# Zero-tile matmuls between score visits, and another spread of the dense units over the first two batches

## The chip, the cores and the metric

The kernel runs on one core of a Trainium2 chip. The metric is the device time of one execution in microseconds (us). The engines are named as the profile names them: PE is TensorE's matmuls and PEld its weight loads, DVE is VectorE, ACT is ScalarE, POOL is GpSimd, SP is SyncE.

## The reference

The input is attention data for 8 batches, 12 heads, 448 positions and 64 elements a head, followed by a dense block with 768 inputs, 2048 hidden elements and 768 outputs. Cut to what is computed:

```python
scores = scale * np.matmul(q, k.transpose(0, 1, 3, 2)) - np.log(S)
attn = 1.0 / (1.0 + np.exp(-scores))
attn_out = np.matmul(attn, v)
x = attn_out.transpose(0, 2, 1, 3).reshape(B * S, H * D)
h = x @ w_in
g = h * (1.0 / (1.0 + np.exp(-beta * h)))
out = g @ w_out
```

The attention uses a sigmoid, not a softmax, so scores can be weighed as soon as they stand. `q`, `k` and `v` are drawn at a tenth of a standard normal deviate, and the output is 3584 x 768 in float32.

## The kernel before

**Names.** Four heads of one batch make a group `g`; a batch has `QPB` = 3 groups, and there are 24 of them. A slot `s` is two heads. The keys of a slot stand in `JF` = 3 full tiles of 128 and one of 64. `visit(g, jt)` (L211) computes the scores of a group's two slots against key tile `jt`: matmuls of `score` (L187) into two PSUM tiles `sco`, and then a sigmoid over each tile by ScalarE (`weigh`, L199), which makes `attnT`. The last key tile of two groups is done in one visit, as in (4, 3, (5,)). `half_visit` (L227) does the same for one half of the queries (224 of 448) and for two key tiles at a time. `attend` (L245) multiplies `attnT` with `v` and lets VectorE copy the result into `xT` (L265). `transpose` (L163) turns a group's `q` or `k` on VectorE, from `raw`, into which `load_one` (L92) brings it by a DMA of GpSimd's queue.

**Dense units.** The dense block is cut into units that fill TensorE's time between visits. `dense1` (L270) is one tile of 128 hidden elements: six matmuls, a sigmoid of ScalarE into `sg` (L284) and a product of VectorE into `gt` (L287). In the first batch it works on half of the positions (224 columns), later on all 448. It needs the column chunk of `w_in` that holds its tile: eight chunks of 256 columns, so two units use one chunk. `dense2` (L291) is 128 output rows by half of the output columns: sixteen matmuls, a copy of VectorE into `osb` (L308), and a store from SyncE's queue when a row is complete. The units stand in one list, `fill`, in a fixed order; `fill_units(n)` takes the next n of them.

**PSUM.** In the first part there are three score tiles of two banks each and two single banks; after `firsts.close()` (L410) two score tiles and four single banks, which the attends and the dense units share. Two score tiles are what one visit fills.

**The order** is written out by hand, and each engine works through its instructions in that order:

- GpSimd's queue loads q and k of the first three groups, `v` of batch 0, the second halves of q, the eight chunks of `w_in`, q and k of group 3, the first half of `w_out`'s columns in two transfers, `v` of batch 1, q and k of group 4, the second half of `w_out`, q and k of group 5.
- TensorE runs 11 matmuls on a tile of zeros, `still`, into the tile `idle` (L370), while the first loads are under way.
- First pass (L386): six `half_visit`s on the first half of the queries of groups 0 to 2, with `attend(0)` cut in two around the last of them. Then the attends of groups 1 and 2, with both half visits of group 0's second half between them (L393 to L408).
- Second pass (L412): four dense units; then for groups 1 and 2 and both halves of a visit: a half visit, half an attend of the group before, three dense units (L417). Then the last attend, the transposes of group 3, and four dense units.
- From there (L433) whole visits. A planner gives each visit a budget of dense work: `spread` names the first eleven, an equal share `rest` follows. Costs are counted as 0.58 for half a `dense1`, 1.13 for a whole one and 2.57 for a `dense2`. A unit is taken when half its cost still fits; a `dense1` of a later batch only when that batch's attends are behind. The transposes of the next group follow the visits with `jt` 1 and 2 (L443), and the attend of a group stands ahead of the next group's first visit (L436).

Of the kernel before, what the change touches and what calls it, by code (L numbers as in the profile page):

```python
# [13 lines left out]
def kernel(  # L14
# [10 lines left out]
    nc = tc.nc  # L25
# [6 lines left out]
    P = 128  # L32
# [4 lines left out]
    JF = S // P  # L37
# [3 lines left out]
    QPB = H // HQ  # L41
# [9 lines left out]
    NQUAD = B * QPB  # L51
# [40 lines left out]
    def load_one(g: int, r: int, c0: int = 0, c1: int = NB):  # L92
        b, t = divmod(g, QPB)
        if g not in raws:
            raws[g] = rawp.tile([P, 2, NB, D], FP16, tag="raw", name="raw")
        nc.gpsimd.dma_start(  # L96
            out=raws[g][:, r, c0:c1].rearrange("p c d -> p (c d)"),
            in_=(q, k)[r][b, HQ * t : HQ * (t + 1)].rearrange("h (p c) d -> (h p) (c d)", c=NB)[
                :, c0 * D : c1 * D
            ],  # L100
        )

    def load_qk(g: int):
        load_one(g, 0)
        load_one(g, 1)
# [4 lines left out]
    def last_base(s: int) -> int:  # L110
        return (s % 2 ^ swapped(s // 2)) * KL

    def load_v(b: int):
        vs[b] = vp.tile([P, H, JF + 1, D], FP16, tag="v16", name="v16")
        rows = v[b].rearrange("h (p c) d -> p h (c d)", c=NB)
        for i in range(HQ):
            nc.gpsimd.dma_start(  # L117
                out=vs[b][i * BLK : (i + 1) * BLK, :, 0:JF].rearrange("p h j d -> p h (j d)"),
                in_=rows[:, :, JF * i * D : JF * (i + 1) * D],
            )  # L120
        if b > 0:
            load_v_last(b)
# [36 lines left out]
    def in_order(b: int, t):  # L159
        t = t.rearrange("p c e -> p (c e)").bitcast(FP32)  # L160
        return t.rearrange("p (q c) -> p c q", c=NB) if b == B - 1 else t

    def transpose(g: int, r: int, c0: int = 0, c1: int = NB):  # L163
        raw = raws[g][:, r]
        if r == 0:
            if g not in qT:
                qT[g] = qTp.tile([P, NB * BLK, PAIR], FP16, tag="qT", name="qT")
            nc.vector.transpose(  # L168
                out=in_order(g // QPB, qT[g][:, c0 * BLK : c1 * BLK]),
                in_=raw[:, c0:c1].rearrange("p c d -> p (c d)").bitcast(FP32),  # L170
            )
            return
        kT[g] = kTp.tile([P, S, PAIR], FP16, tag="kT", name="kT")
        to = kT[g].rearrange("p k e -> p (k e)").bitcast(FP32)
        frm = raw.rearrange("p c d -> p (c d)").bitcast(FP32).rearrange("p (c f) -> p c f", c=NB)
        nc.vector.transpose(  # L176
            out=to[:, 0 : JF * P].rearrange("p (j i q) -> p i j q", j=JF, i=HQ),
            in_=frm[:, 0:NF].rearrange("p (i j) f -> p i j f", j=JF),
        )
        nc.vector.transpose(  # L180
            out=to[:, JF * P :], in_=frm[:, NF:].rearrange("p c f -> p (c f)")
        )
# [62 lines left out]
    def attend(g: int, c0: int, n: int, part=(0, 1)):  # L245
        b, t = divmod(g, QPB)
        if b not in xTs:
            xTs[b] = xTp.tile([P, NHC, S], FP16, tag="xT", name="xT")
        slots = [2 * g + x for x in part]
        avs = [psum["one"].tile([P, S], FP32, tag="one", name="av_ps") for _ in slots]  # L250
        todo = [(s, av, jt) for s, av in zip(slots, avs) for jt in range(JF)]
        for s, av, jt in todo + [(s, av, JF) for s, av in zip(slots, avs)]:
            at = at_tiles.pop((s, jt, c0))
            base, nk = (last_base(s), KL) if jt == JF else (0, P)
            for hh in range(2):
                nc.tensor.matmul(  # L256
                    av[hh * D : (hh + 1) * D, 0:n],
                    vs[b][base : base + nk, 2 * (s % NPAIR) + hh, jt],
                    at[base : base + nk, hh, 0:n],
                    start=(jt == 0),  # L260
                    stop=(jt == JF),
                    tile_position=(base, hh * D),
                )
        for s, av in zip(slots, avs):
            nc.vector.tensor_copy(out=xTs[b][:, s % NPAIR, c0 : c0 + n], in_=av[:, 0:n])  # L265
# [63 lines left out]
    M1_US, M1H_US, M2_US = 1.13, 0.58, 2.57  # L329
# [21 lines left out]
    def fill_units(n: int):  # L351
        for _ in range(n):
            fill[at_fill[0]][2]()
            at_fill[0] += 1
# [4 lines left out]
    with tc.manual_schedule():  # L359
        load_one(0, 0, 0, NH)  # L360
        load_one(0, 1)
        nc.gpsimd.memset(nlogs, NEG_LOG_S)
        nc.gpsimd.memset(dummy, 0.0)
        nc.scalar.activation(out=dummy, in_=dummy, func=AF.Sigmoid, bias=0.0, scale=1.0)

        still = const.tile([P, 512], FP16, name="still")
        nc.vector.memset(still, 0.0)  # L367
        nc.vector.memset(beta_in, 0.0)
        idle = psum["one"].tile([P, 512], FP32, tag="one", name="idle_ps")
        for _ in range(11):  # L370
            nc.tensor.matmul(idle, still[:, 0:P], still, start=True, stop=True)  # L371
        for g in range(1, QPB):
            load_one(g, 0, 0, NH)
            load_one(g, 1)
        load_v(0)
        load_v_last(0)
        nc.sync.dma_start(out=beta_in[0:NDC], in_=moe_beta.rearrange("(c p) -> c p", p=P))
        for g in range(QPB):
            load_one(g, 0, NH, NB)
        for c in range(WCH):  # L380
            load_w_in(c)
        for g in range(QPB):
            transpose(g, 0, 0, NH)
            transpose(g, 1)

        for g in range(QPB):  # L386
            for second in range(2):
                half_visit(g, 0, second)
                if g == QPB - 1:
                    attend(0, 0, QH, (second,))  # L390
        for g in range(QPB):
            transpose(g, 0, NH, NB)
        attend(1, 0, QH, (0,))  # L393
        half_visit(0, QH, 0)
        attend(1, 0, QH, (1,))
        for i in range(P // BLK):
            part = slice(i * BLK, (i + 1) * BLK)
            nc.vector.transpose(out=beta_sb[part], in_=beta_in[:, part])
        attend(2, 0, QH)
        load_qk(3)  # L400
        load_w_out(0, 0)
        load_w_out(1, 0)
        load_v(1)
        load_qk(4)
        load_w_out(0, 1)
        load_w_out(1, 1)
        load_qk(5)
        half_visit(0, QH, 1)  # L408

        firsts.close()  # L410
        share_psum(ctx, 2, 4)
        fill_units(4)  # L412
        for g in range(1, QPB):
            for second in range(2):
                half_visit(g, QH, second)
                attend(g - 1, QH, QH, (second,))
                fill_units(3)  # L417
        attend(QPB - 1, QH, QH)
        transpose(QPB, 0)
        transpose(QPB, 1)  # L420
        fill_units(4)

        visits = [(QPB, jt, ()) for jt in range(JF + 1)]
        for g in range(QPB + 1, NQUAD, 2):
            visits += [(g, jt, ()) for jt in range(JF)] + [(g, JF, (g + 1,))]
            visits += [(g + 1, jt, ()) for jt in range(JF)]
        spread = [3 * M1H_US] * 2 + [M2_US] + [3 * M1H_US] * 2 + [5 * M2_US / 6] * 6

        total = sum(u[0] for u in fill[at_fill[0] :])
        tail = 16 * M1_US + 10 * M2_US  # L430
        rest = (total - sum(spread) - tail) / (len(visits) - len(spread))
        budget, spent = 0.0, 0.0
        for i, (g, jt, also) in enumerate(visits):  # L433
            if jt == 0:
                if g > QPB:
                    attend(g - 1, 0, S)  # L436
                if g + 2 < NQUAD:
                    if g + 2 not in raws:
                        load_qk(g + 2)
                    if (g + 2) % QPB == 0:  # L440
                        load_v((g + 2) // QPB)
            visit(g, jt, also)
            if jt in (1, 2) and g + 1 < NQUAD:  # L443
                transpose(g + 1, jt - 1)
            budget += spread[i] if i < len(spread) else rest
            while at_fill[0] < len(fill):
                cost, ready, _ = fill[at_fill[0]]
                if ready > g or spent + cost / 2 > budget:
                    break
                spent += cost  # L450
                fill_units(1)
        attend(NQUAD - 1, 0, S)
        fill_units(len(fill) - at_fill[0])
# [30 lines left out]
```

## Time and profile before

Three runs took 406.98, 407.15 and 409.64 us; their median is 407.15. The profiled execution took 407.82 us, and its span, from the first to the last instruction, is 406.05 us. Its mean granted TensorE clock is 0.983.

| what | busy us | share of the span | instructions |
|---|---|---|---|
| PE | 395.8 | 97% | 3067 |
| PEld | 201.1 | 50% | 3067 |
| ACT | 236.7 | 58% | 317 |
| DVE | 169.9 | 42% | 335 |
| POOL | 77.2 | 19% | 133 |

The largest groups of TensorE are `dense1` (L276: 864 matmuls, 154.5 us), `dense2` (L298: 896 matmuls, 152.7 us), the scores (L190: 864 matmuls, 54.7 us) and the attends (L256: 432 matmuls, 44.1 us). The sigmoids over scores (L201) are 171 instructions and 160.7 us of ScalarE. The zero matmuls (L371) are 11 and take 4.0 us.

The page has the span in 40 equal slices of some 10 us. A digit is the busy share in tenths, PEclk the TensorE clock that was granted:

```profile
PE   5899999999999999999999999999999999999996
ACT  4778965587534784477643776457843677415400
PEclk9579999999999999999999999999999999999999
DMA  8999999991329402592229212492042200111022
```

TensorE is short of work only in the first slices, the clock is below its full value in slices 1 to 3, and the DMA engines are full for the first 90 us, in which all weights and the first batches are loaded.

The chain that ended last, by engine and by line, is TensorE's for the most part; the DMA share of it lies before 63 us:

```profile
PE 83%; DMA 12%; POOL 2%; issue 1%; DVE 1%; DVEq 0%; POOLq 0%
```

### The profile page before, as it was taken

To read this page: it belongs to the slowest core of one execution; us is meant where nothing else is said; L and a number is where in the kernel's file an instruction comes from. 1 tells how busy PE (TensorE), PEld (TensorE's weight loads), DVE (VectorE), ACT (ScalarE), POOL (GpSimd) and SP (SyncE) were. 2 spreads that over 40 slices of the span, in tenths; PEclk is the share of its full clock that TensorE was granted. 3 is DMA by queue.
4 is the path that set the end of the run, shared out by engine and by line. 5 is a ranking of instruction groups with operands and counts; after the bars stand their busy time and mean duration, and the time that the engine had idled before them with its cause. 6 is when DMAs were issued, how large, how long until landed. Compare 5 with 4: busy or idle time off the path is not lost.

```text
span 406.0 us, 7393 instructions
## 1 busy us (share of the span) xinstructions
PE 395.8 (97%) x3067; PEld 201.1 (50%) x3067; DVE 169.9 (42%) x335; ACT 236.7 (58%) x317; POOL 77.2 (19%) x133
## 2 busy tenths in 40 slices
PE   5899999999999999999999999999999999999996
PEld 2367654444554445444455444544445544555563
DVE  2245353355423653345522454235542365225421
ACT  4778965587534784477643776457843677415400
POOL 7833435420114110420105101321100000000000
PEclk9579999999999999999999999999999999999999
DMA  8999999991329402592229212492042200111022
GB/s 119 151 188 203 180 180 182 196 128 31 85 44 168 75 4 53 115 117 45 39 64 182 56 31 48 77 164 47 0 86 56 62 2 0 40 40 40 0 79 77
DMA packets 48801, 35.09 MB, mean 86 GB/s; under 512 B 28272, under 2 KB 45184, under 8 KB 48768
## 3 DMA queue, kind: packets, MB, share of 16 engines
q0 software_dynamic: 43376, 23.60, 44.8%
q1 hardware_dynamic: 5392, 11.02, 9.8%
q8 instruction: 24, 0.39, 0.4%
q14 instruction: 9, 0.07, 0.1%
HBM read 47.19 MB, written 11.01 MB: 143 GB/s over the span
## 4 chain that ended last, share of the span: by engine, by line
PE 83%; DMA 12%; POOL 2%; issue 1%; DVE 1%; DVEq 0%; POOLq 0%
PE m_ps L298 35%; PE m_ps L276 32%; PE sco L190 9%; PE av_ps L256 8%; DMA w_out<-in_moe_w_out_dram 4%; DMA raw<-in_q_dram 3%; DMA w_in<-in_moe_w_in_dram 3%; DMA v<-in_v_dram 2%; POOL raw L96 1%; POOL w_in L138 1%; POOL v L117 0%; DVE osb L308 0%; POOL w_out L146 0%; DVE qT L168 0%; DVE kT L176 0%
## 5 line engine op out<-in xcount | busy, mean ns | idle before, releaser
L201 ACT ACTIVATE attnT<-sco,nlogs 128x896 f16<-128x896 f32 (+1 forms) x171 | 160.7, 992 | 104.8 <-PE sco L190 104.6
L276 PE MATMUL m_ps<-xT,w_in 128*128 128x448 f16 (+1 forms) x864 | 154.5, 333 | 0.7 <-DVE gt L287 0.7
L298 PE MATMUL m_ps<-w_out,gt 128*128 128x384 f16 (+2 forms) x896 | 152.7, 326 | 0.0
L298 PEld LDWEIGHTS <-gt 128*128 128x128 f16 x896 | 84.6, 98 | 67.5 <-issue 13.7
L276 PEld LDWEIGHTS <-w_in 128*128 128x128 f16 x864 | 81.0, 98 | 71.5 <-issue 15.6
L287 DVE TENSOR_TENSOR gt<-m_ps,sg 128x448 f16<-128x448 f32 (+1 forms) x144 | 79.8, 572 | 85.4 <-ACT sg L284 85.2
L284 ACT ACTIVATE sg<-m_ps,beta_sb 128x448 f32<-128x448 f32 (+1 forms) x144 | 82.2, 596 | 40.0 <-PE m_ps L276 38.9
L308 DVE COPY osb<-m_ps 128x384 f32<-128x384 f32 (+2 forms) x56 | 31.1, 556 | 105.6 <-PE m_ps L298 101.6
L190 PE MATMUL sco<-qT,kT 32*128 32x448 f16 (+3 forms) x864 | 54.7, 350 | 5.3 <-ACT attnT L201 3.4
L96 POOL DMA_DIRECT2D raw<-in_q_dram x27 | 15.0, 555 | 184.3 <-DVE kT L180 180.1
L256 PE MATMUL av_ps<-attnT,v 128*64 128x448 f16 (+3 forms) x432 | 44.1, 354 | 0.0
L265 DVE CAST xT<-av_ps 128x448 f16<-128x448 f32 (+1 forms) x54 | 28.8, 568 | 26.5 <-PE av_ps L256 26.4
L256 PEld LDWEIGHTS <-v 128*64 128x64 f16 (+1 forms) x432 | 19.9, 112 | 25.8 <-issue 19.0
L190 PEld LDWEIGHTS <-kT 32*128 32x128 f16 (+1 forms) x864 | 14.2, 98 | 33.5 <-issue 30.1
L129 POOL DMA_DIRECT2D v<-in_v_dram x32 | 19.5, 616 | 15.2 <-DMA w_out<-in_moe_w_out_dram 6.8
L117 POOL DMA_DIRECT2D v<-in_v_dram x32 | 19.9, 636 | 13.3 <-DMA w_out<-in_moe_w_out_dram 8.1
L168 DVE STREAM_TRANSPOSE qT<-raw 128x448 f32<-128x448 f32 (+1 forms) x27 | 16.5, 615 | 11.6 <-DMA raw<-in_q_dram 11.6
L176 DVE STREAM_TRANSPOSE kT<-raw 128x384 f32<-128x384 f32 x24 | 13.6, 568 | 3.4 <-DMA raw<-in_k_dram 3.4
L96 POOL DMA_DIRECT2D raw<-in_k_dram x24 | 13.2, 551 | 1.2 <-DMA w_in<-in_moe_w_in_dram 1.2
L138 POOL DMA_DIRECT2D w_in<-in_moe_w_in_dram x8 | 6.6, 854 | 0.3 <-DMA v<-in_v_dram 0.3
L371 PE MATMUL idle_ps<-still 128*128 128x512 f16 x11 | 4.0, 532 | 1.2 <-DVE still L367 1.2
L180 DVE STREAM_TRANSPOSE kT<-raw 128x64 f32<-128x64 f32 x24 | 4.9, 202 | 0.0
(13 smaller groups left out, 8.3 us busy)
## 6 DMA issues: line engine op xcount, KB each, us to landing
out_dram<-osb SPq DMA_DIRECT2D x98, 96.0 KB, 2.1
raw<-in_k_dram POOLq DMA_DIRECT2D x24, 224.0 KB, 4.5
raw<-in_q_dram POOLq DMA_DIRECT2D x21, 224.0 KB, 3.6
v<-in_v_dram POOLq DMA_DIRECT2D x32, 144.0 KB, 7.3
w_in<-in_moe_w_in_dram POOLq DMA_DIRECT2D x8, 384.0 KB, 11.1
w_out<-in_moe_w_out_dram POOLq DMA_DIRECT2D x4, 768.0 KB, 14.2
v<-in_v_dram POOLq DMA_DIRECT2D x32, 48.0 KB, 6.3
out_dram<-osb SPq DMA_DIRECT2D x2, 384.0 KB, 2.3
```

The lines of the kernel that those rows point to most:

```text
L96: nc.gpsimd.dma_start(out=raws[g][:, r, c0:c1].rearrange("p c d -> p (c d)"), in_=(q, k)[r][b, HQ * t : HQ * (t + 1)].rearrange("h (p c) d ...
L117: nc.gpsimd.dma_start(out=vs[b][i * BLK : (i + 1) * BLK, :, 0:JF].rearrange("p h j d -> p h (j d)"), in_=rows[:, :, JF * i * D : JF * (i + ...
L129: nc.gpsimd.dma_start(out=vs[b][lo : lo + BLK, :, JF], in_=rows[:, :, c])
L190: nc.tensor.matmul(sco[base : base + nk, hh, u0 : u0 + n], kT[g][lo : lo + BLK, jt * P : jt * P + nk, e], qT[g][lo : lo + BLK, c0 : c0 + n ...
L201: nc.scalar.activation(out=at[:, :, 0:n], in_=sco[:, :, 0:n], func=AF.Sigmoid, bias=nlogs[:, 0:1], scale=MSCALE,)
L256: nc.tensor.matmul(av[hh * D : (hh + 1) * D, 0:n], vs[b][base : base + nk, 2 * (s % NPAIR) + hh, jt], at[base : base + nk, hh, 0:n], start ...
L265: nc.vector.tensor_copy(out=xTs[b][:, s % NPAIR, c0 : c0 + n], in_=av[:, 0:n])
L276: nc.tensor.matmul(m1[:, 0:n], w_in16[:, hc, dc * P : (dc + 1) * P], xTs[b][:, hc, c0 : c0 + n], start=(hc == 0), stop=(hc == NHC - 1),)
L284: nc.scalar.activation(out=sg[:, 0:n], in_=m1[:, 0:n], func=AF.Sigmoid, bias=0.0, scale=beta_sb[:, dc : dc + 1])
L287: nc.vector.tensor_tensor(out=gts[w][:, dc, off : off + n], in0=m1[:, 0:n], in1=sg[:, 0:n], op=ALU.mult)
L298: nc.tensor.matmul(m2, gt[:, dc, t * P : (t + 1) * P], w_out16[:, dc, lo:hi], start=(dc == 0), stop=(dc == NDC - 1),)
L308: nc.vector.tensor_copy(out=osb[:, lo:hi], in_=m2)
```

## The change

Zero matmuls are also run between the first pass's half visits: three after each of the first four, two after the fifth (behind the half of `attend(0)` that follows it), and 13 in place of 11 at the start. In the second pass the three dense units of each of the four rounds become 2, 2, 3 and 3, and two more follow the last round. Group 4's transposes leave the visits (3, 1) and (3, 2) and come behind six dense units that now follow visit (3, 3) by a fixed call. The planner's budgets for the eight visits from (3, 3) on are changed; their sum is the same.

```diff
         idle = psum["one"].tile([P, 512], FP32, tag="one", name="idle_ps")
-        for _ in range(11):
-            nc.tensor.matmul(idle, still[:, 0:P], still, start=True, stop=True)
+
+        def idle_units(n: int):
+            for _ in range(n):
+                nc.tensor.matmul(idle, still[:, 0:P], still, start=True, stop=True)
+
+        idle_units(13)
...
                 half_visit(g, 0, second)
                 if g == QPB - 1:
                     attend(0, 0, QH, (second,))
+                if 2 * g + second < 2 * QPB - 1:
+                    idle_units(3 if g < QPB - 1 else 2)
...
                 half_visit(g, QH, second)
                 attend(g - 1, QH, QH, (second,))
-                fill_units(3)
+                fill_units(1 + g)
+        fill_units(2)
         attend(QPB - 1, QH, QH)
...
-        spread = [3 * M1H_US] * 2 + [M2_US] + [3 * M1H_US] * 2 + [5 * M2_US / 6] * 6
+        spread = [3 * M1H_US] * 2 + [M2_US, 6 * M1H_US + M2_US] + [4 * M2_US / 7] * 7
...
             visit(g, jt, also)
-            if jt in (1, 2) and g + 1 < NQUAD:
+            if jt in (1, 2) and QPB < g < NQUAD - 1:
                 transpose(g + 1, jt - 1)
             budget += spread[i] if i < len(spread) else rest
+            if (g, jt) == (QPB, JF):
+                fill_units(6)
+                spent += 6 * M1H_US
+                transpose(g + 1, 0)
+                transpose(g + 1, 1)
             while at_fill[0] < len(fill):
```

## The prediction

> **What bounds the kernel now.** I read the page first, for the engines' shares; then a table of stretches, for the clock; then the timelines of TensorE, VectorE and ScalarE; then the landings of the weight loads. TensorE is busy 97% of the span, and the list of its waits from 77 us to the end is empty. So what is won or lost before 77 us reaches the end unchanged, and only those 77 us are worked out. First the start, cut at 3.41 us (the columns are length; busy time and count for PE, PEld, DVE, ACT, POOL; granted TensorE clock; DMA):
>
> ```profile
> 4.06:7.48 3.42, 1.75 (x23) 0.71 (x22) 1.53 (x4) 0.08 (x1) 3.38 (x7) 1.00 1.09 156
> 7.48:10.89 3.41, 1.59 (x32) 0.85 (x32) 1.70 (x5) 3.35 (x5) 1.97 (x4) 1.00 1.24 167
> 10.89:14.30 3.41, 1.85 (x26) 0.68 (x27) 0.00 (x0) 3.13 (x4) 1.91 (x5) 0.50 1.83 173
> 14.30:17.72 3.42, 3.42 (x46) 1.50 (x38) 0.39 (x1) 2.79 (x4) 3.42 (x5) 0.50 1.02 124
> 17.72:21.13 3.41, 3.41 (x38) 1.72 (x40) 1.72 (x6) 1.98 (x4) 3.02 (x4) 0.50 1.31 149
> 21.13:24.54 3.41, 3.41 (x38) 1.97 (x35) 1.64 (x7) 1.68 (x2) 1.10 (x2) 0.50 1.40 186
> ```
>
> The clock is full to 10.89 us, half to 24.54, full again after. ScalarE is the busy engine up to 14.3 us, TensorE after that. TensorE's timeline, where it reaches the first dense units:
>
> ```profile
> 22.46 1.07 PE L190 MATMUL sco<-qT,kT 32*128 32x224 f16 x16
> 23.46 2.98 PE L276 MATMUL m_ps<-xT,w_in 128*128 128x224 f16 x24
> 26.38 0.58 PE L190 MATMUL sco<-qT,kT 32*128 32x224 f16 x16
> 26.89 0.69 PE L256 MATMUL av_ps<-attnT,v 128*64 128x224 f16 x8
> ```
>
> Sixteen score matmuls take 1.07 us at half clock and 0.58 at full. What a faster start runs into is in the DMA issues of w_in's second and eighth chunks (issued at 15.0 and 19.9 us; the last figure is the time to landing), and in the wait of GpSimd that the second one ended:
>
> ```profile
> w_in<-in_moe_w_in_dram POOLq DMA_DIRECT2D x1, 384.0 KB, 8.2
> ```
>
> ```profile
> w_in<-in_moe_w_in_dram POOLq DMA_DIRECT2D x1, 384.0 KB, 15.3
> ```
>
> ```profile
> 23.42 0.54 POOL L96 DMA_DIRECT2D raw<-in_k_dram  x1 [1.15 <-DMA w_in<-in_moe_w_in_dram]
> ```
>
> So chunk 2 of 8 lands at about 23.13 us and chunk 8 at 35.16; GpSimd's later waits of this kind end some 2.0 us apart. Last, the second batch's first visits, on TensorE, then VectorE, then ScalarE:
>
> ```profile
> 50.74 0.59 PE L190 MATMUL sco<-qT,kT 32*64 32x448 f16 x8
> 52.01 1.89 PE L276 MATMUL m_ps<-xT,w_in 128*128 128x224 f16 x18 [0.69 <-DVE gt L287]
> 53.83 1.64 PE L256 MATMUL av_ps<-attnT,v 128*64 128x448 f16 x16
> ...
> 64.39 1.09 PE L190 MATMUL sco<-qT,kT 32*64 32x448 f16 x16
> 65.42 1.64 PE L256 MATMUL av_ps<-attnT,v 128*64 128x448 f16 x16
> 66.99 0.91 PE L190 MATMUL sco<-qT,kT 32*128 32x448 f16 x8
> 67.83 2.77 PE L298 MATMUL m_ps<-w_out,gt 128*128 128x384 f16 x16
> ```
>
> ```profile
> 51.04 0.65 DVE L168 STREAM_TRANSPOSE qT<-raw 128x448 f32<-128x448 f32 x1 [4.93 <-DMA raw<-in_q_dram]
> 51.61 0.95 DVE L287 TENSOR_TENSOR gt<-m_ps,sg 128x224 f16<-128x224 f32 x3
> ```
>
> ```profile
> 65.37 1.91 ACT L201 ACTIVATE attnT<-sco,nlogs 128x896 f16<-128x896 f32 x2 [1.68 <-PE sco L190]
> ```
>
> VectorE sat behind group 4's transpose until its q landed; three products waited behind it, and TensorE waited for their PSUM. And two sigmoids, which empty the two score tiles of a visit, take 1.91 us, against 0.51 us for the matmuls that fill them.
>
> **Idle units.** Added are 2 zero matmuls at the start and 2 + 4 x 3 = 14 between visits. In the trace of before they start 0.43 us apart at half clock and 0.216 at full. The first 13 end by 1.2 + 13 x 0.43 = 6.8 us at the latest, where the first scores start (6.79): nothing. A group of three takes 0.65 us. After visits 1 to 4 TensorE waits 1.0, 0.8, 0.75 and 0.8 us for a score tile, so they lie under ScalarE: nothing; without that cover, 5 groups would cost about 3 us. With the clock held, the work from 14 us on runs in half the time. The first pass becomes ScalarE's: its waits of 0.3 us each go, its last sigmoid starts near 17.0 instead of 17.95, and the seventh visit, two attends and the eighth visit follow in about 3.5 us. TensorE reaches the first dense unit near 20.6 us instead of 23.46.
>
> **What is late next: w_in.** Chunk 1 lands near 21.16 us, chunk 2 at 23.13. Units 3 and 4 need chunk 2: 23.13 + 0.04 + 12 matmuls x 0.096 + 0.10 for the change of shape = 24.42, where before the next visit began at 26.38. The gain at this point is 1.96 us, though the half clock cost over 5; being 1.4 us early at the wait, it also survives a start that is up to 1.4 us worse than worked out.
>
> **Units 2, 2, 3, 3, 2.** The same 12 units, 6 x 0.096 us each, in another order. Worked forward with 0.51 (0.64 for the second visit of a group) + 0.62 us between batches, units 5, 7, 9, 11, 13 and 15 start at 25.55, 28.2, 30.6, 31.7, 34.2 and 35.4; their chunks land at 25.13, 27.16, 29.14, 31.12, 33.11 and 35.16. No wait, with 0.2 to 1.5 us to spare; with three units in each batch, unit 7 would wait about 0.5. So the 1.96 us is carried to the second batch: w_out's first half (landed at 45.35) is wanted at 46.07 instead of 48.03, still after it, and visit (3, 3) starts at 48.78 instead of 50.74.
>
> **Group 4's transposes and the spread.** With the costs 0.58 and 2.57 the new budget runs 6.05, 12.10, then 1.469 more at each visit. It gives six dense units and one second-layer unit behind visit (3, 3), then one unit behind (4, 0), (4, 2), (5, 0) and (5, 2), and none behind (4, 1), (4, 3) and (5, 1). The sum is unchanged, so the later visits are as before. Behind (4, 3) stands attend(4); between (4, 1) and (4, 2), and between (5, 1) and (5, 2), TensorE has nothing. No such bare pair is in before's trace. Its price: 0.51 for the first visit, 0.10 to its sigmoids (visit at 61.18, next work 61.69, sigmoids 61.79), 1.91 for the two, and 0.55 from their end to TensorE's next work (67.28 to 67.83) = 3.07 us, against 2 x 0.51 without a wait: 2.05 lost, each time. The lower bound is that TensorE waits only for the first of the two tiles, 1.0 us each; nothing in the trace lets it start sooner. I take 2.05, since the visits of 64.39 and 66.99 show just this wait, with an attend filling most of it.
>
> The chain, from 48.78: visit 0.51; six units 3.45, with 0.3 for PSUM (four banks, and the first product can only follow the visit's two sigmoids); second-layer unit 2.70 (ends 55.8); attend(3) 1.57; visit 0.51; unit 2.70 (60.6); bare pair 3.07; unit 2.70 (66.35); (4, 3), attend(4) and (5, 0), 64.90 to 67.83 in before, 2.93 (69.3); unit 2.70; bare pair 3.07; unit 2.70: 77.75. Before, attend(5) starts there at 76.96. So +0.8 us. What it holds: -1.96 from the start, -0.5 for VectorE (the products no longer stand behind a q that lands at 50.95; the two transposes of group 4 run near 53.8 and are wanted at 57.4), -0.5 since (4, 3) comes at 66.4 and no longer waits for group 5's transposes (64.85), -0.3 of smaller waits and rounding, +4.1 for two bare pairs. GpSimd's queue is not behind any of this: the loads up to group 5 depend on transposes of the first batch alone, and attend(3) finds its v landed (49.7). The profiled execution took 407.82 us for a span of 406.05, 0.67 above the median of 407.15; the difference is added to the median: 407.9.
>
> **A rule against the rows.** In the row, the clock fell at 10.89 us although TensorE's longest gap since 5.14 had been 1.65 us; it was busy 1.59 of 3.41 us. The Trainium skill, "TensorE: Matmul & The Clock Gate", section "HAM oscillation — how this bites in real kernels", asks only that no idle gap be longer than about 3.4 us. By that rule the added zero matmuls would not be needed and a bare pair could never cost clock; by the row, a pair that leaves TensorE busy some 1.5 us of such a stretch may cost half of the next one, 1.7 us. By the rule the sum stays 407.9; by the row it may be 409.6 or 411.3.
>
> **Rivals.** (a) Slower, by the clock: a bare pair falls inside one 3.41 us stretch, TensorE is busy less than about 1.6 us of it, and the clock halves for the next: 1.7 us each, 409.6 for one, 411.3 for two. For it: 7.48 to 10.89 fell at 1.59. Against it: 4.06 to 7.48 had 1.75 and kept its clock, and the stretches must lie just so. (b) The idle units don't hold the clock. TensorE was busy without a gap from 14.3 us and still had to wait until 24.54, so activity alone isn't what is counted. Then the gain of 1.96 goes (409.9), and zero matmuls at half clock (1.28 us a group) outgrow the waits, up to 2 us: 411.9. (c) Faster: the bare pairs cost only 1.0 us each, or less, because the second score tile isn't waited for: 407.9 - 2.1 = 405.8; with no cost at all, 403.8.
>
> **How the numbers follow.** About 1%, 4.1 us, is what a measurement of this kernel can tell from no change. Forecast, 407.9 with 0.7 us either way for the pairs and the PSUM wait: 0.65. (a) 0.15, (b) 0.07, (c) 0.13, most of it between 405 and 407. Even (c) at its end stays above 403.1, so faster by over 1%: 0.02. Slower by over 1% (over 411.2) takes both pairs of (a) or the worse half of (b): 0.06. The range 405.2 to 409.9 holds the forecast, most of (c) and (a) with one pair.
>
> **What would show it.** Clock full from 4 us to the end. TensorE idle before a first dense unit near 21.2 and again before 23.15. Visit (1, 0) of the second pass near 24.4, visit (3, 3) near 48.8, no wait for a product behind it. Then two new waits of TensorE's scores for sigmoids, near 61 to 63 and 72.5 to 74.5, some 2 us each, and attend(5) near 77.7. It is wrong if w_in lands earlier than before, if TensorE isn't at dense unit 3 by 23.1, or if the two waits are under 1 us.

## The result, and the profile after

The changed kernel took 409.37 us (median of 20 runs, 407.80 to 411.74), the kernel before 407.76 us beside it (20 runs, 406.78 to 409.64). The ratio is 1.004, with a 95% interval of 1.0022 to 1.0059: slower by 0.4%, which is less than 1% but clear of zero. The forecast was 407.9, the range 405.2 to 409.9; the median lies inside the range, near its upper end.

The runs fall apart by the mean granted clock of their span:

| mean clock | runs of 20 | time, us | median, us |
|---|---|---|---|
| 1.000 | 5 | 407.80 to 408.40 | 408.26 |
| 0.996 | 10 | 408.88 to 409.97 | 409.37 |
| 0.992 | 5 | 411.40 to 411.74 | 411.60 |

One stretch of 3.41 us at half clock lowers the mean over 407 us by 0.0042, so by their mean these are runs with none, one and two such stretches. The profiled execution of the changed kernel is one with none: 408.26 us, span 406.5.

First the start, as a table of stretches, cut at the same places and with the same columns as that of before (granted clock third from the end):

```profile
7.48:10.89 3.41, 3.12 (x39) 1.17 (x38) 1.51 (x5) 3.35 (x5) 1.69 (x4) 1.00 1.13 150
10.89:14.30 3.41, 3.20 (x42) 1.28 (x42) 0.19 (x2) 3.35 (x5) 2.36 (x5) 1.00 1.85 173
14.30:17.72 3.42, 2.97 (x42) 1.23 (x38) 0.99 (x3) 2.94 (x4) 3.42 (x5) 1.00 1.11 147
17.72:21.13 3.41, 3.16 (x60) 1.90 (x60) 2.77 (x11) 2.34 (x4) 3.35 (x5) 1.00 1.26 158
```

TensorE is now busy 3.1 us of a stretch that held 1.6, the clock stays at full, and ScalarE is busy as long as before (3.35): the zero matmuls lie in waits. TensorE's timeline, where it reaches the dense units, and the DMA issue of w_in's second chunk (issued at 14.77 us):

```profile
20.83 1.32 PE L276 MATMUL m_ps<-xT,w_in 128*128 128x224 f16 x12
22.50 1.32 PE L276 MATMUL m_ps<-xT,w_in 128*128 128x224 f16 x12 [0.35 <-DMA w_in<-in_moe_w_in_dram]
23.76 0.58 PE L190 MATMUL sco<-qT,kT 32*128 32x224 f16 x16
```

```profile
w_in<-in_moe_w_in_dram POOLq DMA_DIRECT2D x1, 384.0 KB, 7.7
```

Two units run, then TensorE waits for chunk 2, which landed at 22.46 us in this execution against 23.13 in that of before. The visit that began at 26.38 begins at 23.76. The first batch's end and the second batch's first visits, on TensorE:

```profile
48.57 0.59 PE L190 MATMUL sco<-qT,kT 32*64 32x448 f16 x8
49.09 3.62 PE L276 MATMUL m_ps<-xT,w_in 128*128 128x224 f16 x36
52.55 2.76 PE L298 MATMUL m_ps<-w_out,gt 128*128 128x384 f16 x16
...
60.02 0.57 PE L190 MATMUL sco<-qT,kT 32*128 32x448 f16 x8
61.69 0.37 PE L190 MATMUL sco<-qT,kT 32*128 32x448 f16 x2 [1.09 <-ACT attnT L201]
62.59 0.57 PE L190 MATMUL sco<-qT,kT 32*128 32x448 f16 x6 [0.53 <-ACT attnT L201]
63.10 2.77 PE L298 MATMUL m_ps<-w_out,gt 128*128 128x384 f16 x16
...
71.60 0.57 PE L190 MATMUL sco<-qT,kT 32*128 32x448 f16 x8
73.27 0.37 PE L190 MATMUL sco<-qT,kT 32*128 32x448 f16 x2 [1.09 <-ACT attnT L201]
74.17 0.57 PE L190 MATMUL sco<-qT,kT 32*128 32x448 f16 x6 [0.53 <-ACT attnT L201]
74.67 2.77 PE L298 MATMUL m_ps<-w_out,gt 128*128 128x384 f16 x16
77.38 1.64 PE L256 MATMUL av_ps<-attnT,v 128*64 128x448 f16 x16
```

Visit (3, 3) starts 2.2 us earlier than before (50.74), and the six units behind it run without a wait. Then two visits stand with nothing between them at 60.02 and again at 71.60: two of the second visit's matmuls run once the first score tile is empty, six once the second is. From the first visit to TensorE's next work it is 63.10 - 60.02 = 3.08 and 74.67 - 71.60 = 3.07 us. attend(5) starts at 77.38 against 76.96 before. On VectorE, group 4's transposes now stand behind the products and wait for nothing:

```profile
53.54 0.64 DVE L168 STREAM_TRANSPOSE qT<-raw 128x448 f32<-128x448 f32 x1
54.10 0.54 DVE L176 STREAM_TRANSPOSE kT<-raw 128x384 f32<-128x384 f32 x1
```

The chain that ended last shows the change of bound in three pieces (start, length, what):

```profile
19.64 15.37 DMA w_in<-in_moe_w_in_dram
...
60.65 1.90 ACT attnT L201 x2
...
72.23 1.90 ACT attnT L201 x2
```

Up to 35 us it runs through the landing of w_in's last chunk, and in each pair through the two sigmoids.

### The profile page after: what moved, and what is told of

Same layout as the page of the kernel before. It is cut to its first block, busy times and chain, and to the rows that moved or that the text cites. A ratio compares the mean times of both kernels' runs of the same rounds, so it can differ in the third digit from the quotient of the medians.

```text
span 406.5 us, 7425 instructions
## 1 busy us (share of the span) xinstructions
PE 396.0 (97%) x3083; PEld 200.7 (49%) x3083; DVE 170.7 (42%) x335; ACT 236.9 (58%) x317; POOL 77.2 (19%) x133
## 4 chain that ended last, share of the span: by engine, by line
PE 88%; DMA 6%; POOL 3%; ACT 2%; issue 0%; DVE 0%; POOLq 0%
PE m_ps L298 37%; PE m_ps L276 34%; PE sco L190 9%; PE av_ps L256 8%; DMA w_in<-in_moe_w_in_dram 4%; ACT attnT L201 2%; DMA v<-in_v_dram 2%; POOL w_in L138 1%; POOL raw L96 1%; POOL v L117 0%; ACT sg L284 0%; DVE osb L308 0%; POOL nlogs L362 0%; POOL dummy L363 0%; POOLq L480 0%
## 5 line engine op out<-in xcount | busy, mean ns | idle before, releaser
L190 PE MATMUL sco<-qT,kT 32*128 32x448 f16 (+3 forms) x864 | 53.4, 340 | 5.2 <-ACT attnT L201 3.5
L256 PE MATMUL av_ps<-attnT,v 128*64 128x448 f16 (+3 forms) x432 | 42.0, 340 | 0.5 <-DMA v<-in_v_dram 0.4
L256 PEld LDWEIGHTS <-v 128*64 128x64 f16 (+1 forms) x432 | 18.9, 107 | 25.1 <-issue 18.1
L373 PE MATMUL idle_ps<-still 128*128 128x512 f16 x27 | 8.4, 450 | 1.2 <-DVE still L367 1.2
L373 PEld LDWEIGHTS <-still 128*128 128x128 f16 x27 | 2.5, 112 | 5.0 <-issue 2.8
```

Of the source, the lines that this page charges most:

```text
L190: nc.tensor.matmul(sco[base : base + nk, hh, u0 : u0 + n], kT[g][lo : lo + BLK, jt * P : jt * P + nk, e], qT[g][lo : lo + BLK, c0 : c0 + n ...
L256: nc.tensor.matmul(av[hh * D : (hh + 1) * D, 0:n], vs[b][base : base + nk, 2 * (s % NPAIR) + hh, jt], at[base : base + nk, hh, 0:n], start ...
```

## The experiments

Theory 1 was that every run pays the two waits between bare pairs of visits, and that in many runs these waits also halve the clock for the next stretch. Theory 2 placed the lost clock in the start, where the zero matmuls would not always hold it. A third view was that the waits only hide waits for loads, so that removing them gives little. The medians, each with that of the kernel before from the same chip (number of runs in brackets). The rows come from three chips, one for each number of runs of before, so medians of rows with different numbers are compared only roughly:

| kernel | median, us (runs) | before beside it | ratio and interval |
|---|---|---|---|
| changed, again | 409.66 (12) | 407.60 (29) | 1.0048, 1.0029 to 1.0067 |
| zero matmuls in both pairs | 407.89 (12) | 407.60 (29) | 1.0004, 0.9991 to 1.0017 |
| units in the pairs | 405.90 (6) | 407.60 (29) | 0.9958, 0.9942 to 0.9973 |
| zero matmuls of the start alone | 408.77 (12) | 407.60 (29) | 1.0024, 1.0006 to 1.0041 |
| changed, without those of the start | 410.57 (10) | 407.90 (26) | 1.0071, 1.0042 to 1.0100 |
| changed, units 3, 3, 3, 3 | 410.55 (11) | 407.90 (26) | 1.0044, 1.0025 to 1.0064 |
| zero matmuls in the first pair | 408.32 (12) | 407.90 (26) | 1.0007, 0.9990 to 1.0024 |
| group 5 early, no bare pair | 405.00 (6) | 407.90 (26) | 0.9920, 0.9897 to 0.9943 |
| zero matmuls on 32 rows in both pairs | 407.80 (12) | 407.85 (17) | 0.9992, 0.9972 to 1.0012 |

### The changed kernel once more

> The changed kernel, once more, for the clock of its runs and for a profile. Theory 1 (bare pairs): every run pays two waits of about 2 us between 60 and 75 us, and most runs also lose clock there; runs of mean clock 1.0 span 406 to 406.7 us, those below 1.0 are 1 to 3.5 us longer; where the profile falls on such a run, its half-clock stretch starts within 3.5 us after one of the two waits. Theory 2 (the start): the clock is lost where the zero matmuls should hold it, so a half-clock stretch lies before 25 us. Theory 3 (neither): it lies somewhere else, or the spans don't go with the clock. Median 409.4.

Three runs of twelve kept the full clock (407.94 to 408.11 us), seven had 0.996, two 0.992. The profile fell on one of the two. Its stretches around both losses:

```profile
4.80:8.21 3.41, 1.14 (x5) 0.29 (x3) 0.26 (x1) 0.00 (x0) 1.67 (x3) 1.00 1.00 127
8.21:11.63 3.42, 3.04 (x35) 1.03 (x35) 1.75 (x6) 1.90 (x2) 2.43 (x4) 0.50 1.37 189
...
73.07:76.48 3.41, 1.79 (x20) 0.63 (x20) 1.70 (x4) 2.27 (x3) 1.32 (x3) 1.00 1.12 240
76.48:79.89 3.41, 3.41 (x12) 1.57 (x11) 0.00 (x0) 1.54 (x2) 3.40 (x6) 0.50 0.97 174
```

And TensorE's timeline, for the cost of the second:

```profile
75.63 0.57 PE L190 MATMUL sco<-qT,kT 32*128 32x448 f16 x6 [0.53 <-ACT attnT L201]
76.13 4.45 PE L298 MATMUL m_ps<-w_out,gt 128*128 128x384 f16 x16
80.51 1.64 PE L256 MATMUL av_ps<-attnT,v 128*64 128x448 f16 x16
```

Both theories show in one execution. The wait of the second pair lies whole in one stretch, which is busy 1.79 us of 3.41; the clock is half in the next, and a second-layer unit takes 80.51 - 76.13 = 4.38 us instead of 2.71: 1.7 us, as the prediction had priced it. The other loss is at the start: here the first k landed 1.9 us later than in the first profile, TensorE waited 2.66 us for its transpose after the 13 zero matmuls, and the stretch was busy only 1.14 us. Visit (3, 3) came 1.5 us late (50.03 against 48.57). That is not the half clock's cost alone, since the first visit was already 1.9 us late by its k (8.59 against 6.72).

### Zero matmuls in both bare pairs

```diff
+            if (g, jt) in ((QPB + 1, 2), (QPB + 2, 2)):
+                idle = psum["one"].tile([P, 512], FP32, tag="one", name="idle_ps")
+                for _ in range(8):
+                    nc.tensor.matmul(idle, still[:, 0:P], still, start=True, stop=True)
             visit(g, jt, also)
```

> The changed kernel with 8 zero matmuls (1.73 us) ahead of the scores of (4, 2) and of (5, 2), that is inside the two waits. Theory 1: the waits stay, since they are the two sigmoids', and TensorE's next second-layer unit starts when it did; the clock is 1.0 in all runs and every run is like the changed kernel's best: span 406 to 406.7, median 408.1 to 408.4 (1.0 to 1.3 below the changed kernel). Theory 2: clock below 1.0 in most runs as before, median 409.4. If the waits were less than 1.7 us the zero matmuls would lengthen the path.

All twelve runs have a mean clock of 0.999 or 1.0 and lie between 407.69 and 408.46 us. The first pair on TensorE:

```profile
59.50 0.57 PE L190 MATMUL sco<-qT,kT 32*128 32x448 f16 x8
60.01 1.90 PE L452 MATMUL idle_ps<-still 128*128 128x512 f16 x8
61.84 0.80 PE L190 MATMUL sco<-qT,kT 32*128 32x448 f16 x8
62.57 2.77 PE L298 MATMUL m_ps<-w_out,gt 128*128 128x384 f16 x16
```

It is 3.07 us from the first visit to the next unit, as without the zero matmuls, so 1.83 us of work cost nothing: the wait is ScalarE's. What went is the lost clock, worth 1.5 to 1.8 us of the median (409.37 and 409.66 to 407.89). It also says that the start loses clock seldom, since the same start stands in these runs. That is against theory 2 as the main cause.

### Zero matmuls in the first pair alone

```diff
+            if (g, jt) == (QPB + 1, 2):
+                idle = psum["one"].tile([P, 512], FP32, tag="one", name="idle_ps")
+                for _ in range(8):
+                    nc.tensor.matmul(idle, still[:, 0:P], still, start=True, stop=True)
             visit(g, jt, also)
```

> The changed kernel with 8 zero matmuls in the first bare pair alone, ahead of (4, 2). Theory 1: runs lose clock at the second pair only: mean clock 1.0 in about half of the runs, 0.996 in the others, 0.992 rare; median between the 407.9 of both pairs filled and the 409.5 of none, 408.2 to 409.3; a half-clock stretch in the profile, if there is one behind 25 us, starts between 73 and 78 us. Rival (one pair alone never tips the clock): all runs at 1.0, median 407.9.

Nine runs of twelve at full clock, three at 0.996, none at 0.992. The median, 408.32, lies between none filled and both filled, as theory 1 had it; the second pair alone lost the clock in at most a quarter of the runs, fewer than the half that was expected, though with twelve runs that is a rough count. The profile fell on a run at full clock, so it doesn't show where the three lost theirs.

### Units in the pairs

```diff
-[M2_US, 6 * M1H_US + M2_US] + [4 * M2_US / 7] * 7
+[M2_US, 6 * M1H_US] + [M2_US] * 3 + [0.0] + [M2_US] * 2 + [0.0]
```

> The changed kernel with its five second-layer units behind (4, 0), (4, 1), (4, 2), (5, 0) and (5, 1) instead of (3, 3), (4, 0), (4, 2), (5, 0) and (5, 2): no bare pair is left. Theory 1: attend(5) starts near 74.3 instead of 77.4, since two waits of 2.05 go and about 1 us comes back as a wait for w_out's last quarter (landing near 62) or group 4's transposes; clock 1.0 in all runs; span about 403.4, median near 405.1, faster than the kernel before by 2 to 3 us. Rival: the waits only hid a wait for the loads of w_out and of group 5, and going round them gives under 1 us beyond the clock: median 407 to 408.2.

405.90 us, faster than before by 0.4% and than the changed kernel by some 3.6 us; all six runs at full clock. It is 0.8 above what was expected, and TensorE's timeline, from three visits and attends with a wait, says why:

```profile
54.75 0.57 PE L190 MATMUL sco<-qT,kT 32*128 32x448 f16 x8 [0.41 <-DVE kT L176]
...
65.12 0.59 PE L190 MATMUL sco<-qT,kT 32*64 32x448 f16 x12 [0.34 <-DVE kT L180]
...
75.70 1.59 PE L256 MATMUL av_ps<-attnT,v 128*64 128x448 f16 x12 [0.66 <-ACT attnT L201]
```

The waits for the transposes of groups 4 and 5 had been counted. Not counted was the last: with no unit behind visit (5, 2), attend(5) stands right behind it and waits for its two sigmoids. attend(5) took from 74.48 to 77.23 us, 1.2 more than its 1.57. Together that is 1.9 of the 4.1 us that two pairs cost, and against the kernel with both pairs filled (407.89) 2.0 us are gained. So the third view fails, and a bare place had in part only been moved to a cheaper spot.

### Group 5 early, and no bare place

```diff
+        load_qk(5)
         load_w_out(0, 1)
         load_w_out(1, 1)
-        load_qk(5)
...
-[M2_US, 6 * M1H_US + M2_US] + [4 * M2_US / 7] * 7
+[M2_US] + [3 * M1H_US] * 2 + [M2_US] * 2 + [0.0] + [M2_US] * 3
...
-                fill_units(6)
-                spent += 6 * M1H_US
+                fill_units(3)
+                spent += 3 * M1H_US
```

> The changed kernel with group 5's q and k loaded ahead of w_out's second half, three dense units behind each of (3, 3) and (4, 0), group 4's transposes behind the first three, and one second-layer unit behind each of (4, 1), (4, 2), (5, 0), (5, 1) and (5, 2). No bare pair, no attend right behind its group's last visit. Theory: group 5's q and k land near 54 instead of 64, w_out's last quarter near 64, where the third second-layer unit wants it near 65; group 4's transposes end near 53.3, a wait of 0.8 us; attend(5) near 74.3, span 402.5 to 403.3, median 404.4 to 405.2, clock 1.0, faster than the kernel before by 2.4 to 3.2 us and than the variant without bare pairs (405.9) by about 1. Rival: with the loads in this order something else is late (w_out's half behind group 5) and it is no better than 405.9.

405.00 us, 404.44 to 405.67, clock at least 0.999: faster than the kernel before by 0.8%, and the best of all. On TensorE:

```profile
53.42 0.57 PE L190 MATMUL sco<-qT,kT 32*128 32x448 f16 x8 [0.41 <-DVE kT L176]
...
74.64 1.64 PE L256 MATMUL av_ps<-attnT,v 128*64 128x448 f16 x16
```

attend(5) starts at 74.64, 2.7 us earlier than in the changed kernel's profile. Between 44 and 80 us the one wait for group 4's transposes is what is left. This order was not run without the added zero matmuls, so how much of its gain needs them is not shown.

### The zero matmuls of the start, alone and taken out

Alone, on the kernel before (units and planner untouched):

```diff
-        for _ in range(11):
+        idle_units(13)
...
+                if 2 * g + second < 2 * QPB - 1:
+                    idle_units(3 if g < QPB - 1 else 2)
```

> The kernel before with the zero matmuls alone (13 and 14), the units and the planner as before. Theory 1: the start gains about 1.6 to 2 us up to visit (3, 1), and all of it goes into a longer wait for the products behind group 4's transpose (its q lands near 51.4) and for group 5's transposes (near 64.9); attend(5) near 77, clock 1.0, median 407.0 to 408.0, the same as before. Rival: the gain of the start is carried through: attend(5) near 75, median about 405.8.

408.77 us, a little slower than before and 0.8 above the upper end of what theory 1 expected. TensorE's timeline where the products stand behind group 4's transpose, that transpose on VectorE, and the stretches there:

```profile
52.32 3.27 PE L276 MATMUL m_ps<-xT,w_in 128*128 128x224 f16 x18 [2.57 <-DVE gt L287]
```

```profile
51.34 0.65 DVE L168 STREAM_TRANSPOSE qT<-raw 128x448 f32<-128x448 f32 x1 [6.81 <-DMA raw<-in_q_dram]
```

```profile
48.38:51.79 3.41, 1.37 (x14) 0.53 (x12) 0.45 (x1) 1.35 (x2) 3.41 (x6) 1.00 0.99 138
51.79:55.21 3.42, 2.89 (x16) 2.37 (x16) 2.51 (x8) 0.89 (x2) 2.01 (x4) 0.50 1.01 134
```

The transpose starts when its q has landed, at 51.34 us against 51.04 before. So the early start does go into the wait for the products, which grows from 0.69 to 2.57 us, and in this execution that longer wait in turn halves the clock: attend(5) starts at 78.32, against 76.96 before. Over the runs this explains the slower median only in part: the six runs at 0.999 or 1.0 have a median of 408.1 and the six below it 409.2, but the fastest of all twelve, 407.12, had 0.991. The kernel before says the same of its own start: among its runs beside these experiments two kept the full clock, and at 407.22 and 407.90 they were not faster than the rest (medians 407.60 and 407.85).

Taken out of the changed kernel:

```diff
-        idle_units(13)
+        for _ in range(11):
+            nc.tensor.matmul(idle, still[:, 0:P], still, start=True, stop=True)
...
-                if 2 * g + second < 2 * QPB - 1:
-                    idle_units(3 if g < QPB - 1 else 2)
```

> The changed kernel without its added zero matmuls (11 at the start, none between visits); units and planner as changed. Theory 1: the half clock of the kernel before is back up to about 24.5 us, visit (1, 0) of the second pass starts near 26.4 instead of 23.8 and visit (3, 3) near 50.7 instead of 48.6; no load is waited for after that, so the 2 us reach the end: attend(5) near 79.5, at full clock behind 25 us a span of 408.5, median 410.4 to 411.5, that is 1 to 2 above the changed kernel. Rival: the start doesn't matter since w_out and group 5's loads set attend(5): median within 0.5 of the changed kernel's 409.4 to 409.7.

410.57 us. Visit (1, 0) of the second pass and visit (3, 3) start where theory 1 had them, the latter 2.1 us later than in the changed kernel's first profile:

```profile
26.14 0.58 PE L190 MATMUL sco<-qT,kT 32*128 32x224 f16 x16
...
50.67 0.59 PE L190 MATMUL sco<-qT,kT 32*64 32x448 f16 x8
```

The times alone show it less clearly: the interval, 1.0042 to 1.0100, overlaps that of the changed kernel, 1.0029 to 1.0067. Six of the ten runs have a mean clock of 0.983, which is four stretches, as many as the start of before lost. If all four are the start's, their median of 409.9 is to be set against 408.26 for the changed kernel at full clock: 1.6 us. One run doesn't fit: it had a mean clock of 1.0 and took 411.0 us. There is no trace of it, so what it lost is open. In the profile both pairs lost the clock; the stretches around the first:

```profile
61.83:65.24 3.41, 1.79 (x20) 0.46 (x18) 1.54 (x3) 2.02 (x3) 1.30 (x3) 1.00 1.15 210
65.24:68.65 3.41, 3.41 (x13) 1.55 (x12) 0.36 (x2) 1.79 (x2) 1.75 (x3) 0.50 1.50 188
```

### Three units in each round

```diff
-                fill_units(1 + g)
-        fill_units(2)
+                fill_units(3)
```

> The changed kernel with three dense units in each of the four rounds of the second pass, as before, and none behind the last round. Unit 7 then asks for w_in's fourth chunk near 26.2 us, which lands near 27.1. Theory 1: a wait of 0.5 to 1 us there, carried to the end: attend(5) near 78, median 0.5 to 1.0 above the changed kernel's, 410.0 to 410.6. Rival: the wait only takes the place of one for a later chunk or of ScalarE's, and the median stays within 0.3.

410.55 us, 0.9 to 1.2 above the changed kernel's two medians. The seventh unit waits for its chunk:

```profile
27.13 0.75 PE L276 MATMUL m_ps<-xT,w_in 128*128 128x224 f16 x6 [0.95 <-DMA w_in<-in_moe_w_in_dram]
```

Visit (3, 3) starts at 49.20, 0.6 us later than in the changed kernel's first profile, and the three runs at full clock have a median of 408.85 against 408.26. So 2, 2, 3, 3, 2 is worth about 0.6 us, and most of the wait of 0.95 is not taken up later. The times as a whole don't settle it: this chip is another one, and against before the two ratios are nearly the same (1.0044 and 1.0048).

### Zero matmuls on 32 rows

On the kernel with zero matmuls in both pairs, so that these use 32 of the 128 rows:

```diff
-                    nc.tensor.matmul(idle, still[:, 0:P], still, start=True, stop=True)
+                    nc.tensor.matmul(
+                        idle, still[0:BLK, 0:P], still[0:BLK], start=True, stop=True, tile_position=(0, 0)
+                    )
             visit(g, jt, also)
```

> The changed kernel with 8 zero matmuls in each of the two bare pairs, on 32 rows of the array instead of 128: the same 1.73 us of busy time, a quarter of the array. If busy time alone is what holds the clock, this is like the kernel with full zero matmuls: clock 1.0 in all runs, median 407.7 to 408.1. If the share of the array counts, the pairs' stretches hold too little (1.8 us of scores and second-layer unit, and a quarter of 1.6 more): clock 0.996 or 0.992 in several of the runs, median 408.3 to 409.5. In both cases the waits are as long as before.

407.80 us, 407.45 to 408.45, all twelve runs at 0.999 or 1.0. Work on a quarter of the rows holds the clock in a pair as well as work on all of them.

## Why the prediction was right or wrong

**The start.** Right. The gain ended at w_in's second chunk: 26.38 to 23.76 is 2.6 us, of which 0.7 is luck, since this execution's chunk landed earlier; the rest is the 1.96 forecast. The last chunk, for which the prediction saw no wait and 0.2 us to spare, did bind (35.01 us), and took back about 0.3. Visit (3, 3) was forecast at 48.78 and started at 48.57.

**The pairs.** Right in place and size: 3.07 forecast for each, 3.08 and 3.07 measured. The PSUM wait of 0.3 us among the six units wasn't there. attend(5) was forecast at 77.75 and started at 77.38. At full clock the changed kernel took 408.26 us, 0.5 above the median of before, where the sum had 0.8.

**The clock.** Here the sum was short. Rival (a), a bare pair that halves the clock, had its mechanism, its place and its price (1.7 us) right, but a chance of 0.15. In 24 of the 32 runs of the changed kernel at least one stretch lost the clock, and with both pairs filled none of 24 did, so that the median lies 1.1 us above the median of the runs at full clock. It stayed within the range only because the range had been drawn wide enough for (a) with one pair; the 0.65 had gone to 407.9 with 0.7 us either way. The step that went wrong was "the stretches must lie just so". In the first profile of the changed kernel, which kept its clock, the stretches cut both waits:

```profile
58.98:62.39 3.41, 1.99 (x17) 0.77 (x16) 0.56 (x1) 2.11 (x3) 0.07 (x1) 1.00 1.24 209
72.63:76.04 3.41, 2.24 (x17) 1.06 (x17) 0.78 (x3) 2.87 (x4) 2.34 (x5) 1.00 1.11 250
```

Where a stretch held the whole wait it was busy 1.79 or 1.80 us, and the clock fell. How often that happens can be estimated from the rows. The wait with the two matmuls in its middle takes 1.09 + 0.37 + 0.53 = 1.99 us, and if the stretches lie at random it falls whole into one of 3.41 us in (3.41 - 1.99) / 3.41 = 0.42 of the cases. The 2.05 us of the prediction would have given 0.40, far above the 0.15 for one pair or both. In the 32 runs 8 had no stretch at half clock, 17 one and 7 two; two independent chances of 0.42 would give 11, 16 and 6. That agrees in size only: the pairs stand a fixed 11.58 us apart (60.02 and 71.60) and so aren't independent, and at least one of the losses was the start's.

**Rival (b)**, that the zero matmuls don't hold the clock, was not seen: the one start that lost it had its 13 zero matmuls behind it, and then a wait of 2.66 us for a late k with none in it. **Rival (c)**, cheaper pairs, was not seen either. **The rule against the rows:** the Trainium skill's "TensorE: Matmul & The Clock Gate", section "HAM oscillation — how this bites in real kernels", would let a pair pass, since no idle gap nears 3.4 us. The longest gap in the pair that lost it was 1.1 us, and the clock fell. The rows decide.

**Why the early start bought nothing.** The three parts are tied: the zero matmuls alone end in a longer wait for the products; the moved transposes remove that wait, but to cover the loads the planner put three more half units and one whole unit ahead of group 4 and left two places bare, which cost 4.1 us. With the places filled and group 5 loaded earlier the kernel ends 2.9 us ahead of the one before (405.00 against 407.90).

## What to carry to other kernels

Between two visits that fill all score tiles, TensorE needs at least the time of the sigmoids that empty them: spread fill work by that, place by place, and not by a sum over several visits. A start that is made faster gains only up to the next load, so the loads and the order behind it have to move with it. A wait well under the clock's stretch can still cost half of the next stretch; a row of runs, each with its clock, shows it where one profile may not.

## What the runs showed of the hardware

Where a stretch's busy time could be read beside a pair or a wait, the clock fell after 1.14, 1.37, 1.59, 1.67, 1.79 and 1.80 us of 3.41 (1.67 in the start without the added zero matmuls, 1.79 in three executions), and stayed after 1.99 and 2.24. No stretch that began at full clock was seen between 1.80 and 1.99. It also stayed after 1.75 us once, in the start of before, of which 1.08 were zero matmuls; what tells that case apart is open. Coming back was not alike either: after a pair, one stretch full of dense work was enough, and in the second execution's start one with 3.04 us of scores and zero matmuls, while in the start of before three full stretches of scores and attends at half clock (14.30 to 24.54 us) were needed. Whether it is the kind of work that makes the difference there was not tried.
